# Lag products of two neighbouring channels at once, 64 rows by 40 columns, with reordered channels and a new instruction order

## The chip, the core and the metric

The kernel runs on one core of a Trainium2 chip. The metric is the device time of one execution in microseconds; lower is better. The core has a matrix engine (PE, with its weight loads listed as PEld), a vector engine (DVE), a scalar engine (ACT), GpSimd (POOL) and the SP queue, which in this kernel issues all transfers, one after the other.

## The reference

Two branches are computed from the same input x (2048 tokens, 512 channels) and mixed by a gate.

```
g = sigmoid((x * gate_w).sum(-1, keepdims=True))
a = attention(x)      # 32 heads of 16, 4 segments of 512: causal softmax inside a segment,
                      # plus a linear memory of the segments before; then @ wo
b = ssm_conv(x)
out = g * a + (1 - g) * b

# ssm_conv, for each of 512 channels d, with 128 complex states n:
dt = exp(log_dt);  A = A_re + 1j*A_im;  dB = dt * (B_re + 1j*B_im);  C = C_re + 1j*C_im
P[d,n,l] = exp(dt*A * l)
K[d,l] = real( sum_n C[d,n] * P[d,n,l] * dB[d,n] )         # a kernel of 2048 lags
y = causal convolution of x and K along the tokens (by FFT) + x * Dskip
```

The lags l are bfloat16 numbers in the reference, so only some of the 2048 differ.

## The kernel before, in words

**Order.** The program first builds a list of 1853 operations, each with its engine, its function and its dependences. A long string, `ORDER`, then says in which order they are put on the engines' queues, which buffer each takes, and for moves out of PSUM whether ACT (mark `a`) or DVE (mark `v`) does them. `replay` assigns the buffers, `emit` works out the semaphore waits. Every engine runs its own list strictly in that order; transfers all stand in SP's list.

**Attention.** For each segment s and group hg of eight heads: projections to q and k, scores in five pieces (A0, B0, C, A1, B1), each 128x2048, that always use PSUM banks 0 to 3, one exponential for each piece on ACT (80 in all, L1080), products with v, a division, the memory's part, and a transposition. The other four banks serve all other work.

**Lag kernel.** `ssm_prep` transposes the six parameter arrays (three products of eight transposes, moved out of PSUM by `evac`) and computes z = exp(dt*A); `ssm_powers` squares it nine times; `ssm_cb` makes C*dB (and, with Dskip, a diagonal). `tables(c)`, for each group c of 128 channels, builds by complex products on DVE (L1175, L1178, L1182) two tables: F with the powers z^f for 20 exponents and G with C*dB*z^g for 32 exponents. The wanted values are K at lag f+g = sum over n of G[n,g]*F[n,f] for every channel: the *lag products*. States n lie on the 128 partitions, so each channel is one product with 32 columns of weights (G) and 20 moving columns (F), for the real and the imaginary part added up in PSUM. Four channels run in four strips of 32 columns of the array (`tile_position`). Half of a group's results fill one bank; `evac` moves them to the tile `kex`, and four transfers of 40 KB bring `kex` into `KTT`, from which the spectra are made. A table stores channel pairs next to each other: its place is `(dl//2)*2*N + 2*e + dl%2` for channel dl and exponent e.

**Convolution.** `x_level1` transforms x and writes it to memory (`Zd`). `tail(half)`, for channels 0 to 255 (a) and 256 to 511 (b) and each of 16 frequency groups t: load constants (CT 192 KB, CD 320 KB) and a slice Zx, product X, swap of its halves by two transfers, product K from `KTT` and CD, product Y on DVE, inverse product V, and a transfer into V2. At the end, for 16 token groups, products with wo and the last inverse step are added in PSUM and mixed by DVE (L1331, L1336), then stored.

All matrix products are recorded at the helper's line L698, moves out of PSUM at L226 (ACT) and L227 (DVE), transfers at L222.

Of the kernel before, what the change touches and what calls it, by code (L numbers as in the profile page):

```python
# [7 lines left out]
ACT = mybir.ActivationFunctionType  # L8
# [358 lines left out]
15/0 9/0 10/1 205/0 0/0 23/0/1 24v 29/0 30/0 31/10 193/0 33/7 54/1 57/5 21/0 189/0 1/0 14/2 1226/0 38/1 34 7/0  # L367
1234/4/0 1244/1/1 12/1 35 36 39/2 37/3 32/4 45/7 1242/2 44/5 13/4 11/3 40/6 46/8 190 41 17/0 20/0 58v/0 1232/3 55/7
27/5/0 42 43 50/12 48/0 47 1245a 18/0 5/0 191 61/1 16/0 59/0 51/13 62v/0 60 63 49/9 25/6/2 71/0 588/0 56a 196/0 73/2
53/0 2/0 72 83/1 52 200/1/0/0 85/3 26v 84 74v/2 1233a 98v/1 97/4 1235a 65/2 3/0 95/1 250/7/1/1 391/1 212/6 66/5 197/0  # L370
96 86v/3 67 201a 87 1243a 1246 109/3 64 107/3 108 122v/4 110a/5 77/0 6/0 213a 121/6 251a 28v 202 75 79/7 99 1247/1 88
1236 119/1 203/2/0 100 76 173/0 120 204a 176/2 219/0/1 220 198/0 174/3 131/1 178/1 589/3 175/0 994v/0 252 133/2 590
132 78 134v/6 221 255/2/0/1 253/0/1 240/0/0 111 112 241 256 257 192/0 377/0 996v 143/3 1310/0 1260/3/1 144/4 254a 997v
145 206/1 242 177 157/3 91/0 208/2 228/0/2 995v 229 1000/1 181/1 155/0 1261a 999 1258/0 123 124 199/0 1012/0 179/3 156
209a 214/3/1/0 210/2 230 1001 158v/7 1005 998v/0 159 1002 1003/1 1004 207a 211a 146v/8 223/0/3 224 1248/1/0 135 160
1259a 225 89/2 167v/9 258 1250/2 147 1249a 168 1009/1 222/0 1251a 136 236/0/1 4/0 237 148 226 227 235/1 169 231 1011
337/2/2 90 1013 1008 232/3 1020 1021/0 238 262/0/3 103/6 215 263 1252 338a 1262 101/0 233 1227/2/0 239 216 1022 102
264 1010 243 234/0 244 217 1265/3/1 1014 1015/0 245/4 115/1 1228a 113/2 266/0/2 1023 267 1229/0 246 1024/1 114
293/2/2/2 1266a 268 265/3 247 799/0 1016 271/0/1 272 592/0 1025 294a 1230a 1006/0 8/0 800/1 273 1231 383/0/0/0 384a
269 1237/2/0 125/0 279/0/0 280 801 295 1017 1018/1 378/0 379 270 274 1007 275/0 1019 1263/1 1032 127/4 1033/0 281  # L380
296/0/0 283/0/3 284 1264a 276 1267 297a 1238a 381 285 1026 1239/1 334/2/1/1 1255/0/1 335a 1240a 307/0/2 308 218/2/0
259 1256a 278/1 277/1 1034 309 1029 1027/1 1030/0 282 286 287 1253/0 1268/0 1241 1254a 298/3/1/0 260/0 299 1031 1035
303/0/1 1036/0 304 1028 443/0/1 305 1286/2/0 802 1287a 320/0/0 321 1037 126 1043/2/1 1044 1045 380 444a 1289/1 1257
288/1 137/2 1046 139/2 300 138 1047v 339/0/0/1 398/3 194 289 151/3 385 322 340 312/0/3 1290/2/1 313 180 399a 341 290
1292/3 248/0 149/0 182 249v/0 314 1293v 1038/1 1039 150 336 1040 1041 1056a/0 1053v/0 1055v 1052v 1054v 1058/1 342
1057 306/0 1284/3 1291a 1042a 1285a 591 324/0/1 325 310 311 291/2 386/1/0 315 382/1 1288 1059 1274/3/0 1070/0 68v/0
1063 1060 1061/1 1062 69 1066 1294 1067/1 104v/2 326 346/0/2 347 387a 319/1 323 327 328 329/2 1051/0 80v/1 316/5 1069
292a 348 396/2 1068 1073/1 330 350/0/3 1275a 351 1276/3 397a 1071 1300/2/1 352 317 1078 355/0/0 152a/5 331/1 1072 81
1277a 356 1302/1 349/3 353 1278 1079/0 1301a 318 1281/2/0 1279/0 357 363/0/1 364 354 358 1303a 1074 116v/4 105 106
1076/1 1080 153 1081 92a/7 392/1 365 393a 1282a 1280a 1075 359/1 367/0/2 368 70 1082/0 1304 93 369 360 1283 490/1/2/2  # L390
1271/2/1 301 361/0 1272a 94 302/0 1084 1083 1269/3 154 405/0/3 406 1077 343 1050 22/0 1090 1048 362/2 366 370 1270a
1307/3/0 1091/0 371 1049 1273 344 1088/1 407 447/0 332/0 1092 409/0/0 410 1087 1089 1064/0 491a 117 118 82 1308a 394/1
1065 411 1297/3/1 333a 395a 1085/1 372/3 422/0/2 423 1298a 1295/0 408/1 412 1094/0 1093 1305/3 1296a 1095 424 1086
140v/6 440/0/1/1 388/0 163/0 389 141 1330/0 1306a 441a 1317/1 426/0/3 427 1101/3/0 1299 1096/0 1097 1102 1103 1104 373
195 374 164a/3 448/2/1/0 1309 165 492 128v/9 345 390/1 261 428 414/0/1 1105a 161/2 449 450 415 493/3/2 416 413 1098
1099 494a 1100a 1318/0 1331/1 1113a/0 1319/0 162 442 472/0/0 473 1332/1 1358/2 417 142 129 421/2 425 429 1320/3/0 474
170v/8 171 451 375/0 430 1108 130 1321a 1114v/0 1111v 1119/0 1118 1110v 1112v 1120 1115 1116/1 1109 376a 455/0/1 418/4
1117 1106 166 1128/0 1125/1 1323 1107 1124 1121 431/0 456 457 1322 1127 1126 1333/3/2 541/0/0 1129 1131/1 1136 542a
1122/0 543/1 1130 459/0/2 460 172 1345/1 461 419 432 1132 1324/0/0 1325a 433/0 464/0/3 1137/1 1334a 465 803 458/0
1326/0 1344/0 462 1327/2/0 1138 466 400/3/0/1 463 1371/0 420 1328a 401 476/0/1 1134/1 1133 471/1 477 467 1335 1336  # L400
# [1039 lines left out]
```

## Time and profile before

| | |
|---|---|
| median of 3 runs | 306.34 us (306.05 to 309.47) |
| the profiled execution | 307.74 us |
| its span, first to last instruction | 305.9 us |
| PE busy | 255.6 us (84%) |
| DVE busy | 277.6 us (91%) |
| ACT busy | 256.9 us (84%) |
| mean granted PE clock | 0.964 |
| moved by transfers | 47.91 MB |

Busy time is the time in which at least one instruction of the engine was in flight; on PE it counts the length of pipelined products and is no measure of how full the array was. Times in the rows are microseconds from the start of the span, except means, which are nanoseconds.

### The profile page before, as it was taken

Reading aid. Unit: us, or ns where it says so; the run is one execution under the profiler, and the core shown is the slowest. Engines: PE = TensorE matmul, PEld = TensorE weight load, DVE = VectorE, ACT = ScalarE, POOL = GpSimd, SP = SyncE. Lnnn points to the kernel's source line nnn. Section 1 sums busy time; section 2 is a strip of 40 time slices with the busy share of each in tenths; the row PEclk is TensorE's granted clock in tenths of the full one; section 3 lists DMA queues with packets and bytes.
Section 4 is the critical chain, followed back from the end, with each engine's and each line's share of the span. In section 5 each row is a group of like instructions: output and inputs, shape, how many; then the busy total and the mean of one; then the engine's idle time right before and its main releaser. Section 6 shows DMA issues by size and latency. Waiting matters only on the chain.

```text
span 305.9 us, 10281 instructions
## 1 busy us (share of the span) xinstructions
PE 255.6 (84%) x4334; PEld 177.4 (58%) x4367; DVE 277.6 (91%) x690; ACT 256.9 (84%) x305; POOL 3.3 (1%) x10
## 2 busy tenths in 40 slices
PE   1667779888777859998999998999999998899990
PEld 1423335546453636677666675677577666688870
DVE  1999996999999889999999988898899899989992
ACT  2899997999999987887999999899999999993000
POOL 2000000000000000000000000000000000000000
PEclk9999975999799998999999999999999999999996
DMA  6996361432133723564655557667686676742243
GB/s 150 286 181 164 72 155 36 139 105 79 51 93 88 247 67 121 132 190 142 188 168 175 183 168 216 204 189 222 201 257 185 194 249 197 246 113 81 88 150 91
DMA packets 55502, 47.91 MB, mean 157 GB/s; under 512 B 22688, under 2 KB 50336, under 8 KB 55456
## 3 DMA queue, kind: packets, MB, share of 16 engines
q1 hardware_dynamic: 55456, 47.26, 52.9%
q8 instruction: 34, 0.56, 0.8%
q14 instruction: 12, 0.10, 0.1%
HBM read 29.02 MB, written 6.29 MB: 115 GB/s over the span
## 4 chain that ended last, share of the span: by engine, by line
ACT 40%; PE 25%; DVE 18%; DMA 7%; issue 4%; SPq 4%; DVEq 0%
PE psum L698 24%; ACT sb L1080 22%; ACT sb L226 11%; SPq L222 4%; DVE sb L1336 4%; DVE sb L1331 3%; DMA sb<-c_DNM 3%; ACT sb L806 3%; DVE sb L1285 2%; DMA sb<-sb 2%; DVE sb L1175 2%; DMA sb<-in_A_x_dram 2%; DVE sb L1178 1%; DVE sb L1182 1%; DVE sb L227 1%
## 5 line engine op out<-in xcount | busy, mean ns | idle before, releaser
L698 PE MATMUL psum<-sb 128*128 128x17 bf16 (+10 forms) x4246 | 249.3, 224 | 35.5 <-ACT sb L1080 19.4
L698 PEld LDWEIGHTS psum<-sb 128*128 128x128 bf16 (+3 forms) x4279 | 171.1, 96 | 111.6 <-ACT sb L1080 36.0
L1080 ACT ACTIVATE sb<-psum 128x2048 bf16<-128x2048 f32 x80 | 151.4, 1892 | 4.0 <-PE psum L698 3.4
L226 ACT ACTIVATE sb<-psum 128x512 bf16<-128x512 f32 x156 | 88.2, 611 | 14.1 <-PE psum L698 13.7
L1175 DVE TENSOR_TENSOR sb<-sb 128x512 bf16<-128x512 bf16 (+3 forms) x52 | 34.0, 662 | 1.4 <-DMA sb<-sb 1.4
L227 DVE CAST sb<-psum 128x512 bf16<-128x512 f32 (+1 forms) x46 | 30.8, 674 | 4.0 <-PE psum L698 3.5
L1178 DVE TENSOR_TENSOR sb<-sb 128x512 bf16<-128x512 bf16 (+3 forms) x52 | 34.0, 659 | 0.0
L1182 DVE TENSOR_TENSOR sb<-sb 128x512 bf16<-128x512 bf16 (+3 forms) x52 | 33.7, 664 | 0.2
L1092 DVE TENSOR_TENSOR sb<-sb 128x1024 bf16<-128x1024 bf16 (+1 forms) x40 | 22.8, 580 | 2.0 <-ACT sb L1080 1.7
L1285 DVE TENSOR_TENSOR sb<-sb 128x1024 bf16<-128x1024 bf16 x32 | 21.7, 679 | 1.3 <-ACT sb L226 0.7
L1331 DVE SCALAR_TENSOR_TENSOR sb<-sb 128x256 f32<-128x256 bf16 x32 | 14.2, 480 | 0.3 <-DMA sb<-in_A_x_dram 0.3
L1055 DVE TENSOR_TENSOR sb<-psum,sb 128x256 bf16<-128x256 f32 x32 | 13.3, 417 | 0.3
L1336 DVE SCALAR_TENSOR_TENSOR sb<-psum,sb 128x256 bf16<-128x256 f32 x32 | 13.3, 479 | 0.0
L806 ACT ACTIVATE sb<-sb 128x512 f32<-128x512 f32 x18 | 11.7, 658 | 0.0
L1052 DVE RECIPROCAL sb<-psum 128x16 f32<-128x16 f32 x32 | 7.9, 248 | 0.9 <-PE psum L698 0.9
L227 DVE COPY sb<-psum 128x1024 bf16<-128x1024 bf16 x4 | 2.7, 687 | 6.3 <-PE psum L754 6.3
L1132 DVE TENSOR_TENSOR sb<-psum,sb 128x512 bf16<-128x512 f32 x12 | 8.2, 687 | 0.2
L960 ACT ACTIVATE sb<-psum 128x512 bf16<-128x512 bf16 x12 | 7.4, 615 | 0.4 <-PE psum L957 0.4
L1011 ACT ACTIVATE sb<-sb 128x512 bf16<-128x512 bf16 x12 | 7.6, 633 | 0.0
L807 DVE TENSOR_TENSOR sb<-sb 128x256 f32<-128x256 f32 x18 | 7.5, 423 | 0.0
L808 DVE SCALAR_TENSOR_TENSOR sb<-sb 128x256 f32<-128x256 f32 x18 | 7.4, 414 | 0.0
L754 PE MATMUL psum<-sb 128*128 128x128 bf16 x24 | 2.6, 290 | 5.3 <-DMA sb<-c_ident 5.3
(67 smaller groups left out, 102.2 us busy)
## 6 DMA issues: line engine op xcount, KB each, us to landing
sb<-c_DNM SPq DMA_DIRECT2D x32, 320.0 KB, 3.7
sb<-c_DNM SPq DMA_DIRECT2D x32, 192.0 KB, 2.9
sb<-sb SPq DMA_DIRECT2D x84, 64.0 KB, 2.6
sb<-in_A_x_dram SPq DMA_DIRECT2D x9, 512.0 KB, 4.6
scr_Z<-sb SPq DMA_DIRECT2D x16, 256.0 KB, 2.3
sb<-scr_Z SPq DMA_DIRECT2D x32, 128.0 KB, 3.2
sb<-sb SPq DMA_DIRECT2D x32, 128.0 KB
out_dram<-sb SPq DMA_DIRECT2D x8, 256.0 KB, 2.2
```

Of the source, the lines that this page charges most:

```text
L226: fa = lambda e: e.activation(dst(), src(), ACT.Copy)
L227: fd = lambda e: e.tensor_copy(dst(), src())
L698: mm = lambda e, o_, l, r_, st, sp, **kw: e.matmul(o_, lhsT=l, rhs=r_, start=st, stop=sp, skip_group_check=True, **kw)
L806: op("ACT", ("As", 512), lambda e, sq=sq, Z=Z: e.activation(ap(sq, n=512), ap(Z, n=512), ACT.Square), r=[Z], w=[sq], key=PW[h] + PWS * k)
L1080: o = op("ACT", ("Ax", 2048), lambda e, P=P, pT=pT: e.activation(ap(pT, n=2048), ap(P, n=2048), ACT.Exp, scale=0.25), r=[P], w=[pT])
L1092: op("DVE", ("V2", 128 * nb), lambda e, pT=pT, dims=dims: e.tensor_tensor(ap(pT, dims=dims + [[1, 128]]), ap(pT, dims=dims + [[1, 128]]), ...
L1175: op("DVE", ("V2" if n > 1 else "V1", 256 * n), lambda e: e.tensor_tensor(run(tile, ne, dst, 1), run(tile, ne, src, sstep), ap(pw, cl * 51 ...
L1178: op("DVE", ("V2" if n > 1 else "V1", 256 * n), lambda e: e.tensor_tensor(run(t2, n, 0, 1), run(tile, ne, src, sstep), ap(pw, cl * 512 + 2 ...
L1182: op("DVE", ("V2" if n > 1 else "V1", 256 * n), lambda e: e.tensor_tensor(D_(), D_(), ap(t2, n * 128, [[-n * 128, 2], [2 * n, 64], [1, 2 * ...
L1285: op("DVE", ("V2", 1024), lambda e, Y=Y, XAB=XAB, K3=K3: e.tensor_tensor(ap(Y, dims=[[512, 2], [1, 512]]), ap(XAB, dims=[[512, 2], [1, 512 ...
L1331: op("DVE", ("V1", 256), lambda e, xd=xd, b4=b4: e.scalar_tensor_tensor(ap(xd, n=256), ap(xns[b4 // 4], (b4 % 4) * 512 + half * 256, n=256 ...
L1336: op("DVE", ("V1", 256), lambda e, ou=ou, b2=b2, j=j, b4=b4, P=P, xd=xds[j]: e.scalar_tensor_tensor(ap(ou, (2 * b2 + j) * 256, n=256), ap( ...
```

## The change

- A lag product now takes a pair of neighbouring channels: 64 columns of weights (32 exponents of both channels, contiguous) and 40 moving columns (20 exponents of both). The result is 64 by 40, of which the halves that mix the two channels are not wanted. Two pairs run in two strips of 64 columns. There are 512 products instead of 1024, with twice the result columns.
- A group fills four PSUM banks, eight channels each, instead of two. `evac` moves a bank with both column parities, 320 elements on each partition, so there are 16 such moves instead of 8. The wanted half is picked by the transfers out of `kex`, which read every second partition. `kex` is twice as large, with one buffer instead of two.
- So that the picked half lies as before, the channels are reordered in the tables: in each block of 64, places 2s and 2s+1 hold channels s and 32+s. The move of the transposed parameters, the exponential of log_dt, the load of Dskip (now four) and the diagonal row carry that order.
- `ORDER` is another list with 1864 operations (not shown: 97 lines). Nearly all neighbourhoods are alike, but many operations stand some places earlier or later, and 80 moves out of PSUM or copies are new or on another engine than before; of the lag moves 13 are on ACT and 3 on DVE (5 and 3 before).

```
-    kexP = mkpool("kex", 1280, 2)
+    kexP = mkpool("kex", 2560, 1)
...
-    S.dma(lambda: ap(dskT, n=4), lambda: B_Dskip.rearrange("(k p) -> p k", p=128), 1024, w=[dskT], key=9, slow=True, q=LQ)
+    for j in range(4):
+        S.dma(lambda j=j: ap(dskT, n=4, p0=64 * (j // 2) + j % 2, np_=32, pstep=2), lambda j=j: B_Dskip.rearrange("(k p) -> p k", p=128)[32 * j:32 * j + 32, :],
+              256, pw=[dskT], key=9, slow=True, q=LQ)
...
-            S.evac(lambda T=T: ap(T, n=1024), lambda P=P: ap(P, n=1024), 1024, r=[P], w=[T], psum16=True)
+            S.evac(lambda T=T: ap(T, dims=[[64, 16], [1, 2], [2, 32]]), lambda P=P: ap(P, dims=[[64, 16], [32, 2], [1, 32]]), 1024, r=[P], w=[T], psum16=True)
...
-        op("ACT", ("Asx", 512), lambda e: e.activation(ap(dt, n=512), ap(ldt, n=512), ACT.Exp), r=[ldt], w=[dt])
+        op("ACT", ("Asx", 512), lambda e: e.activation(ap(dt, dims=[[64, 8], [1, 2], [2, 32]]), ap(ldt, dims=[[64, 8], [32, 2], [1, 32]]), ACT.Exp), r=[ldt], w=[dt])
...
-        for hf in range(2):
+        for b in range(4):
             P = S.ps()
-            for sl0 in range(0, 16, 4):
-                def f(e, P=P, hf=hf, sl0=sl0):
-                    for sl in range(sl0, sl0 + 4):
+            for s0 in range(8 * b, 8 * b + 8, 4):
+                def f(e, P=P, b=b, s0=s0):
+                    for s in range(s0, s0 + 4):
                         for cc in range(2):
-                            for dq in range(4):
-                                dl = 32 * dq + 16 * hf + sl
-                                i = mm(e, ap(P, sl * NF, n=NF, p0=32 * dq, np_=32), ap(G, (1 - cc) * GPL + (dl // 2) * 2 * NG + dl % 2, [[2, NG]]),
-                                       ap(F, cc * FPL + (dl // 2) * 2 * NF + dl % 2, [[2, NF]]), cc == 0, cc == 1, tile_position=(0, 32 * dq))
+                            for h in range(2):
+                                i = mm(e, ap(P, (s - 8 * b) * 40, n=40, p0=64 * h, np_=64), ap(G, (1 - cc) * GPL + (32 * h + s) * 2 * NG, n=64),
+                                       ap(F, cc * FPL + (32 * h + s) * 2 * NF, n=40), cc == 0, cc == 1, tile_position=(0, 64 * h))
                     return i
-                op("PE", c_pe("C", *[20] * 8), f, r=fr + gr + [F, G], pw=[P], acq=[kex])
-            S.evac(lambda hf=hf: ap(kex, 16 * hf, [[32, NF], [1, 16]]), lambda P=P: ap(P, dims=[[1, NF], [NF, 16]]), 320, r=[P], pw=[kex])
+                op("PE", c_pe("C", *[40] * 4), f, r=fr + gr + [F, G], pw=[P], acq=[kex])
+            S.evac(lambda b=b: ap(kex, 8 * b, [[640, 2], [32, NF], [1, 8]]), lambda P=P: ap(P, dims=[[1, 2], [2, NF], [40, 8]]), 320, r=[P], pw=[kex])
         for dq in range(4):
             S.dma(lambda dq=dq: ap(KTT, (4 * c + dq) * 160, n=160),
-                  lambda dq=dq: ap(kex, n=640, p0=32 * dq, np_=32), 40960, r=[kex], pw=[KTp[c // 2]])
+                  lambda dq=dq: ap(kex, dq % 2 * 640, n=640, p0=64 * (dq // 2) + dq % 2, np_=32, pstep=2), 40960, r=[kex], pw=[KTp[c // 2]])
...
-    S.evac(lambda: ap(drowT, n=512), lambda: ap(PR, n=512), 512, r=[PR], w=[drowT], key=200)
+    S.evac(lambda: ap(drowT, dims=[[64, 8], [32, 2], [1, 32]]), lambda: ap(PR, dims=[[64, 8], [1, 2], [2, 32]]), 512, r=[PR], w=[drowT], key=200)
```

More of the change, by code (lines that the diff above doesn't have):

```diff
@@ new lines @@
+1505a 708a 656 662/2/1/1 625 457 626 627 631 1598/0 1490 1500/1/2 663 1489 1501a 664 807/1 604/1 555 636/0/3 603
+1624/2 1221/3 1222 1483 989/0 1524/1 1224/1 1223v 188 1512/0 1503 1502 637 1225 704/2/1/0 1226a 1493/0 632/2 686/0/2
+687 1494/3/0 547 596/0 633 665 634/0 1517/1/1 638 635/0 639 1470 669/0/1 1518v 1510/1 1420/0 1622/2 1609/4 1234 705v
+1235 1495a 643 1506/1 644 1530/1/0 645/3 646 670 647 706 1531a 671 1507/2/1 673/0/3 1513/3/0 1508a 585/0/4/0 1419/0
+819/2 1514v 614/3/0/0 586 1596/0 1515 1623/0 587 588 1236 1509 674 734/0/0 1233 820v 615 1525/1 672/0 735 1516
```

179 lines of the change are left out of this document (87 added, 92 removed).

## The prediction, on record before the result was known

> **What bounds the kernel now.** I read the page first, then the busy time by stage, then the chain of waits and the groups by shape.
>
> ```profile
> span 305.9 us, 10281 instructions
> PE 255.6 (84%) x4334; PEld 177.4 (58%) x4367; DVE 277.6 (91%) x690; ACT 256.9 (84%) x305; POOL 3.3 (1%) x10
> ACT 40%; PE 25%; DVE 18%; DMA 7%; issue 4%; SPq 4%; DVEq 0%
> 0.00:24.00 24.00, 11.99 (x106) 7.41 (x108) 17.39 (x51) 17.36 (x33) 1.98 (x8) 1.00 0.84 207
> 24.00:100.00 76.00, 60.30 (x1089) 34.88 (x1101) 72.76 (x185) 73.56 (x94) 0.65 (x1) 0.91 0.35 98
> 100.00:165.60 65.60, 57.82 (x1175) 41.50 (x1169) 61.99 (x151) 57.02 (x73) 0.00 (x0) 0.97 0.54 159
> 165.60:272.20 106.60, 100.14 (x1729) 71.63 (x1739) 98.71 (x240) 103.75 (x103) 0.66 (x1) 1.00 0.66 201
> 272.20:300.10 27.90, 25.33 (x268) 22.00 (x266) 26.77 (x68) 5.24 (x7) 0.00 (x0) 1.00 0.37 112
> ```
>
> The last five rows are stretches of the span; after the length come the busy times of PE, PEld, DVE, ACT and POOL. I cut at the starts of the 24th, the 40th and the 80th exponential (L1080) and at DVE's last work. No engine is the bound of the whole: from 24 to 100 us ACT is idle for 2.4 us and DVE for 3.2; from 100 to 165.6 DVE paces (3.6 idle, ACT 8.6); from 165.6 to 272.2 ACT paces (2.9 idle, DVE 7.9); at the end DVE (1.1 idle). The last 5.8 us are the way out of the last stores. A microsecond added to the pacing engine of a stage is worth about one, on another engine less.
>
> How the ACT stages run:
>
> ```profile
> 73.58 0.97 ACT sb L226 x2
> 74.55 1.78 ACT sb L1080
> 269.82 1.88 ACT L1080 ACTIVATE sb<-psum 128x2048 bf16<-128x2048 f32 x1
> 272.20 1.88 ACT L1080 ACTIVATE sb<-psum 128x2048 bf16<-128x2048 f32 x1 [0.50 <-PE psum L698]
> 265.17 0.70 DVE sb L227
> 266.20 0.60 DVE sb L227
> ```
>
> A PSUM move of 512 costs ACT 0.97/2 = 0.48 and DVE 0.60 when others follow. All exponentials use the same four PSUM banks, so with nothing put between them two of them stand 2.38 apart, 0.5 of it idle.
>
> **The lag products.** They are the 32-column products:
>
> ```profile
> L698 PE MATMUL psum<-sb 128*32 128x20 bf16 x1024 | 10.1, 177 | 1.1 <-issue 0.9
> L698 PE MATMUL psum<-sb 128*128 128x17 bf16 x1280 | 44.2, 171 | 0.5 <-DVE sb L227 0.2
> 64.14:65.15 1.01, 1.01 (x127) 1.00 0.27 95
> 74.19:75.18 0.99, 0.99 (x42) 1.00 0.24 57
> 102.98 1.11 PE psum L698 x25
> 136.18 3.30 PE psum L698 x124
> 140.84 2.07 PE psum L698 x134
> 180.73 4.80 PE psum L698 x190
> ```
>
> The window at 64.14 holds only lag products: 127 in 1.01 us, 8.0 ns each. Four of them, in four column strips, stand side by side, so a round of four takes 32 ns; 1024 are 256 rounds, 8.2 us. The window at 74.19 holds the 17-column products that use the whole array, and there one takes 0.99/42 = 24 ns. After the change there are 512 products but only two side by side: again 256 rounds. So the halved count doesn't halve the time. The new round (64 columns of weights, 40 moving) is not in the trace. From below it is bounded by 24 ns (6.1 us in all), from above by transposes with 128 columns of weights and 128 moving:
>
> ```profile
> 118.34 0.39 PE L957 MATMUL psum<-sb 128*128 128x128 bf16 x4
> L957 PE MATMUL psum<-sb 128*128 128x128 bf16 x48 | 4.7, 219 | 0.2
> ```
>
> Four take 0.39 of which the last itself lasts 0.22, so they start 57 ns apart (14.6 us in all). The 17-column row is the nearer in moving size: I take 27 ns, 6.9 us, a gain of 1.3. Only part lies on the chain: the groups quoted at 102.98, 136.18, 140.84 and 180.73 have 473 products, by the shapes some 380 of them lag products (3.0 us); a sixth of that is **-0.5**, at 24 ns -0.7, at 57 ns +2.3.
>
> The Trainium skill (TensorEngine Tiling, Overview and Tiling Modes) speaks against the change: a weight width up to 32 lets four column tiles run, up to 64 two, so twice the width is half the tiles; by it the PE time stays 8.2 us and the term is 0. The trace agrees with the four-fold half of it (8.0 ns each).
>
> **The additional PSUM moves.** Half of each product is thrown away, so a channel group fills four banks instead of two: 16 moves of 320 instead of 8.
>
> ```profile
> L226 ACT ACTIVATE sb<-psum 128x320 bf16<-128x320 f32 x5 | 2.3, 457 | 0.4 <-PE psum L698 0.4
> L227 DVE CAST sb<-psum 128x320 bf16<-128x320 f32 x3 | 1.5, 487 | 0.1
> L226 ACT ACTIVATE sb<-psum 128x512 bf16<-128x512 f32 x150 | 85.3, 614 | 13.6 <-PE psum L698 13.3
> L227 DVE CAST sb<-psum 128x512 bf16<-128x512 f32 x43 | 29.3, 688 | 3.9 <-PE psum L698 3.5
> L227 DVE COPY sb<-psum 128x1024 bf16<-128x1024 bf16 x4 | 2.7, 687 | 6.3 <-PE psum L754 6.3
> ```
>
> The order's marks say which engine takes each: ACT 13 instead of 5, DVE 3 as before. Of the 457 ns some 0.13 overlap the next instruction as in the 512 row (614 against 0.48), so ACT gets 8 x 0.32 = 2.6. The new order pays with other moves: of those of 512, DVE takes 50 instead of 43 (+4.2), ACT 143 (-3.3); one of 1024 and two small copies go the other way. Over the kernel DVE gets +3.1, ACT +0.9.
>
> By stage, counting between the same three exponentials in both orders with these prices: before the 24th ACT +0.3, DVE -0.9; from there to the 40th ACT +3.0, DVE +2.3 (a table product is drawn forward); to the 80th ACT -1.9, DVE +2.3; behind it DVE -0.6. Taking the pacing engine of each stage: **+0.3**, **+2.3**, then a choice, then **-0.6**. In the third stage ACT paces, but its 1.9 us less don't come back whole: three exponentials now follow another with nothing between, one before, at 0.5 idle each, and others get less than 0.5 between them; summed as the larger of 2.38 and 1.77 plus what stands between, ACT's road from the 40th to the 80th is 103.5 before and 103.7 after. Bounds: -1.9 and DVE's +2.3; I take **+0.9**, nearer to ACT.
>
> **The reordering in the tables.** The parameter moves now write every second element. On DVE 1024 bf16 take 687 ns, as long as 512 f32, so two elements pass at a time; if the step breaks that, one of them takes about 0.6 more. Three moves: one goes to ACT, one has time, the first is on the path of the start: 0 to +0.6, **+0.4**. The exponential of dt and the diagonal row are written or read with a step by engines that already take one element at a time: nothing, else some tenths. The Trainium skill (VectorE: DVE Perf Modes, What auto-detection actually checks) has the paired mode only for 16-bit tensors with step 1; by it the term would be the full +0.6. No step of two in such a move is in this trace.
>
> **The queue.** One small load of Dskip becomes four:
>
> ```profile
> 90.61 0.60 SPq L222 DMA_DIRECT2D sb<-in_B_Dskip_dram  x1
> 8.39 2.32 SPq L222 DMA_DIRECT2D sb<-in_gate_w_dram  x1
> 111.88 0.60 SPq L222 DMA_DIRECT2D sb<-sb  x1
> sb<-sb SPq DMA_DIRECT2D x1, 40.0 KB, 1.9
> 113.91 4.60 PE L698 MATMUL psum<-sb 128*128 128x256 bf16 x54 [1.95 <-ACT sb L1080]
> 116.23 1.09 ACT L226 ACTIVATE sb<-psum 128x512 bf16<-128x512 f32 x2 [2.36 <-PE psum L698]
> 112.79 0.69 DVE L1175 TENSOR_TENSOR sb<-sb 128x1024 bf16<-128x1024 bf16 x1 [1.36 <-DMA sb<-sb]
> 116.86 0.69 DVE L1285 TENSOR_TENSOR sb<-sb 128x1024 bf16<-128x1024 bf16 x1 [0.73 <-ACT sb L226]
> ```
>
> Three more issues of 0.6 on SP; one of them and the load of gate_w (2.3) now stand ahead of the input x of the first transform. What is queued behind them (x, wq, wk) is needed around 13 to 17 us; x would be issued near 8 us and take 4.6, just in time. Nothing for that, as ACT and DVE have the powers' chain to do until then; 1 us if it is late.
>
> The other rows are a wait that the order removes. The only 40 KB transfer in the window from 111.86 is the last lag move of group 1; issued at 111.88, landed 1.9 later, at 113.8, and PE starts the first kernel spectrum (K, half a) at 113.91 after 1.95 idle. ACT and DVE wait for that (2.36, 0.73); DVE's 1.36 wait is for a power's copy from the same queue. Before, that last move stood behind the swap of the first X; now the four stand ahead of it, so that after the last PSUM move near 106 they are issued by about 109.7 and land by 111.6; the power's copy stands earlier too. DVE gets back 1.36 + 0.73: **-2.1** (0 if another transfer is late instead, -2.4 with ACT's).
>
> Against this, constants come later in the new order.
>
> ```profile
> sb<-c_DNM SPq DMA_DIRECT2D x32, 192.0 KB, 2.9
> PEld psum L698 <- DMA sb<-c_DNM: 1.5, 2, 0.9
> PE psum L698 <- DMA sb<-c_DNM: 1.4, 3, 0.8
> ```
>
> The 192 KB loads land after 2.9; 8 of 32 have under 1 us of ACT's and DVE's work between the place of their issue and their product, before 3. The shortfalls of all transfers of the tail against their landing times add up to 52 instead of 42, a quarter more; a quarter of the waits above and of the like, **+0.4** (0 to +2). The single kex buffer costs nothing: groups are over 25 us apart and a lag transfer lands in about 2; the four moves out of it still carry 40 KB each.
>
> **Sum.** 0.3 + 0.4 + 2.3 - 2.1 - 0.5 + 0.9 - 0.6 + 0.4 = +1.1. The profiled execution took 307.74 (its span 305.9 and 1.8 around it), which makes 308.8; it lies 1.4 above the median of the runs, 306.34, from which the forecast is **307.4**. Bounds of the terms, all at one end: -3.0 and +10.2.
>
> **Rivals.**
> - *Constants late.* The place is PE's wait at the X products of the tail. Five more loads are issued at their use; at 2.9 each that is 14.5, with half covered by products already queued +7, instead of 0.4: 314.0. For it: SP is one queue in order and stands behind waits. Against it: in the trace PE and PEld wait only 2.9 in all for c_DNM, though 12 loads were close already. It decides once such waits pass about 8 us.
> - *DVE takes every stage.* Then the +2.3 of the third stage counts in full and the removed wait returns elsewhere: 307.4 + 1.4 + 2.1 = 310.9. For it: DVE is 91% busy and gets 3.1 more. Against: 7.9 idle in the third stage.
> - *The new order is simply tighter.* ACT's -1.9 comes back, -2.4 at 113, no other wait, and nothing for steps and constants: 307.4 - 2.8 - 0.3 - 0.8 = 303.5. For it: ACT has less to do where it paces. Against: the three exponentials with nothing between.
> - *No gain on PE.* A round of two stays 32 ns or more, up to 57: +0.5 to +2.8, 308 to 310; it is inside the forecast's range.
>
> **Chances.** Forecast (with the last rival) 0.50, constants 0.13, DVE 0.19, tighter 0.18. Two per cent, about what a measurement of this kernel tells from no change, are 6.1 us: 300.2 to 312.5. Beyond the upper end lie most of the first rival and little of the second, 0.15; below the lower end a tail of the tight order, 0.06; within 0.79. Range 302.5 to 313.0; the forecast's own 305 to 310.
>
> **What would show it.** Lag products: 512 in about 7 us, pairs 27 ns apart. The 320 moves: 13 on ACT at 0.46, 3 on DVE at 0.49. Parameter moves on DVE at 1.1 to 1.3 instead of 0.69. No wait near 114 us ahead of the first K. DVE busy near 280. It is wrong if the exponentials from the 40th to the 80th take over 110 us, if PE waits over 8 us for c_DNM, or if a round of lag products passes 50 ns.

## The result and the profile after

| | before | after |
|---|---|---|
| median of 20 runs, us | 306.76 (304.92 to 309.47) | 304.69 (303.27 to 306.36) |
| ratio, 95% interval | | 0.9922 [0.9899, 0.9945] |
| profiled execution, us (span) | 307.74 (305.9) | 304.81 (303.0) |

The change is 0.8% faster, 2.1 us. The forecast was 307.4, 0.3% slower than the median known then: its sign was wrong, its range (302.5 to 313.0) held the time. On another chip the change itself came out at 0.9948 [0.9910, 0.9985]. The ratios compare undisturbed executions alone, so a ratio need not be the quotient of two medians over all executions.

The page of after, then the stretches cut at its own 1st, 24th, 40th and 80th exponential and at VectorE's last work:

```profile
span 303.0 us, 9317 instructions
PE 260.7 (86%) x3855; PEld 176.8 (58%) x3855; DVE 280.6 (93%) x694; ACT 258.4 (85%) x309; POOL 3.3 (1%) x10
PE 31%; DVE 27%; ACT 26%; DMA 5%; issue 5%; SPq 4%; DVEq 0%; ACTq 0%
```

```profile
0.00:25.55 25.55, 12.47 (x88) 6.88 (x89) 19.79 (x56) 18.43 (x32) 1.98 (x8) 0.98 0.85 209
25.55:99.94 74.39, 64.12 (x923) 35.15 (x923) 72.49 (x184) 73.31 (x92) 0.65 (x1) 0.89 0.34 96
99.94:163.22 63.28, 57.38 (x981) 41.54 (x981) 61.09 (x140) 59.48 (x81) 0.00 (x0) 1.00 0.59 166
163.22:269.50 106.28, 101.59 (x1608) 71.08 (x1606) 101.17 (x251) 102.51 (x101) 0.66 (x1) 1.00 0.69 205
269.50:296.97 27.47, 25.11 (x268) 22.15 (x266) 26.06 (x66) 4.64 (x6) 0.00 (x0) 1.00 0.31 92
```

Set against the same five stretches of before (24.0, 76.0, 65.6, 106.6 and 27.9 long), the 24th exponential comes at the same time, and the stretch to the 40th is 2.3 us shorter. VectorE's columns say how. It works 3.0 us more in all, and is idle 16.4 us up to its last work instead of 22.5 (by stretch 5.8, 1.9, 2.2, 5.1, 1.4 after; 6.6, 3.2, 3.6, 7.9, 1.1 before). More work and less waiting: -6.1 + 3.0 and 0.2 more at the end is the -2.9 of the spans.

The groups that the change touches:

```profile
L698 PE MATMUL psum<-sb 128*64 128x40 bf16 x512 | 9.2, 186 | 0.1
L226 ACT ACTIVATE sb<-psum 128x320 bf16<-128x320 f32 x13 | 5.5, 466 | 0.4 <-PE psum L698 0.3
L227 DVE CAST sb<-psum 128x320 bf16<-128x320 f32 x3 | 1.5, 486 | 1.0 <-PE psum L698 1.0
L226 ACT ACTIVATE sb<-psum 128x512 bf16<-128x512 f32 x143 | 81.9, 624 | 8.2 <-PE psum L698 7.8
L227 DVE CAST sb<-psum 128x512 bf16<-128x512 f32 x50 | 33.5, 682 | 1.5 <-PE psum L698 1.3
L227 DVE COPY sb<-psum 128x1024 bf16<-128x1024 bf16 x3 | 3.2, 1083 | 1.0 <-PE psum L756 1.0
```

The third field is the idle time ahead of the group. Ahead of ScalarE's 512 moves it fell from 13.6 to 8.2, ahead of VectorE's from 3.9 to 1.5; ahead of the lag products from 1.1 (0.9 of it "issue") to 0.1.

One warning on the pair of profiles. The granted clock in 40 slices, of before, of after, and of an experiment (e8 below) whose program is that of before up to about 95 us:

```profile
PEclk9999975999799998999999999999999999999996
```
```profile
PEclk9997978999996999999999999999999999999996
```
```profile
PEclk9998879999999997999999999999999999999996
```

Before's profile was granted 0.7 and 0.5 in its slices from 38 to 53 us, and its 21st exponential starts at 89.6; the same program starts it at 87.3 in e8 and at 88.2 in e17. So the profile of before stands about one microsecond above its median (307.74 against 306.76), and of the 2.9 us between the two spans some 2 are the change's.

A second difference of clock lies where the change gains most. The clock falls to half for 3.4 us or a multiple of it, at other places in other executions. In before's profile it is half from 113.5 to 116.9 us, in that of after nowhere between 99.5 and 297:

```profile
103.05:117.40 14.35, 10.07 (x188) 6.26 (x189) 11.54 (x36) 11.78 (x15) 0.00 (x0) 0.88 0.36 99
102.95:114.64 11.69, 8.56 (x126) 5.29 (x125) 11.46 (x35) 11.65 (x17) 0.00 (x0) 1.00 0.60 161
```

These are the stretches from the 25th to the 29th exponential, before and after; the third figure from the end is the granted clock. Three traces in the order of after that have 3.4 us of half clock between 107 and 117 us (e3, e15, e16 below) take 63.0 to 64.2 us from the 24th to the 40th exponential, against 63.3 in after and 65.6 in before. So most of the 2.3 us stays when both have such a stretch, but a difference of one or two microseconds between two single traces can be the clock alone.

### The profile page after: what moved, and what is told of

The parts are those of the page before. It is cut to its first block, busy times and chain, and to the rows that moved or that the text cites. A ratio compares the mean times of both kernels' runs of the same rounds, so it can differ in the third digit from the quotient of the medians.

```text
span 303.0 us, 9317 instructions
## 1 busy us (share of the span) xinstructions
PE 260.7 (86%) x3855; PEld 176.8 (58%) x3855; DVE 280.6 (93%) x694; ACT 258.4 (85%) x309; POOL 3.3 (1%) x10
## 4 chain that ended last, share of the span: by engine, by line
PE 31%; DVE 27%; ACT 26%; DMA 5%; issue 5%; SPq 4%; DVEq 0%; ACTq 0%
PE psum L698 30%; ACT sb L1082 11%; ACT sb L226 10%; DMA sb<-sb 4%; SPq L222 4%; DVE sb L1337 4%; DVE sb L227 4%; DVE sb L1332 3%; DVE sb L1286 3%; DVE sb L1094 3%; ACT sb L808 3%; DVE sb L1177 2%; DVE sb L1184 2%; DVE sb L1180 2%; DMA sb<-in_B_log_dt_dram 1%
## 5 line engine op out<-in xcount | busy, mean ns | idle before, releaser
L698 PE MATMUL psum<-sb 128*128 128x17 bf16 (+11 forms) x3767 | 254.7, 233 | 24.0 <-ACT sb L1082 11.7
L226 ACT ACTIVATE sb<-psum 128x512 bf16<-128x512 f32 (+2 forms) x158 | 88.9, 618 | 8.6 <-PE psum L698 8.1
L227 DVE CAST sb<-psum 128x512 bf16<-128x512 f32 (+1 forms) x53 | 34.9, 671 | 2.4 <-PE psum L698 2.3
L1094 DVE TENSOR_TENSOR sb<-sb 128x1024 bf16<-128x1024 bf16 (+1 forms) x40 | 22.5, 573 | 0.4 <-ACT sb L1082 0.4
L756 PE MATMUL psum<-sb 128*128 128x128 bf16 x24 | 2.7, 279 | 5.0 <-DMA sb<-c_ident 4.6
L959 PE MATMUL psum<-sb 128*128 128x128 bf16 x48 | 4.9, 227 | 2.2 <-ACT sb L226 2.2
```

Source lines behind the costliest of these rows:

```text
L226: fa = lambda e: e.activation(dst(), src(), ACT.Copy)
L227: fd = lambda e: e.tensor_copy(dst(), src())
L698: mm = lambda e, o_, l, r_, st, sp, **kw: e.matmul(o_, lhsT=l, rhs=r_, start=st, stop=sp, skip_group_check=True, **kw)
L1094: op("DVE", ("V2", 128 * nb), lambda e, pT=pT, dims=dims: e.tensor_tensor(ap(pT, dims=dims + [[1, 128]]), ap(pT, dims=dims + [[1, 128]]), ...
```

## The experiments

Two theories at the outset. **A**: the new order alone brings the gain, the products nothing. **B**: the products bring it, on TensorE. Start of some exponentials in the traces, to place each gain and loss (us):

| | 1st | 21st | 25th | 29th | 33rd | 37th | 80th | span |
|---|---|---|---|---|---|---|---|---|
| before | 24.2 | 89.6 | 103.1 | 117.4 | 131.7 | 154.1 | 272.2 | 305.9 |
| after | 25.6 | 89.2 | 103.0 | 114.6 | 130.5 | 151.5 | 269.5 | 303.0 |
| e1 old products, new order | 25.3 | 89.3 | 105.4 | 117.6 | 133.0 | 159.7 | 278.1 | 311.4 |
| e9 the same, half the products | 25.0 | 88.0 | 101.3 | 112.8 | 128.6 | 149.6 | 269.8 | 303.2 |
| e12 after, two transfers back | 25.4 | 88.9 | 102.6 | 114.2 | 132.2 | 153.2 | 270.9 | 304.4 |
| e17 before, two transfers forward | 24.4 | 88.2 | 101.7 | 114.3 | 128.6 | 150.7 | 268.2 | 302.2 |

### Products and order taken apart (e1, e2)

```diff
 e1: ORDER of after, operations of before
-lag%d: 8 x 16 products of 64x40, 4 moves of 320
+lag%d: 8 x 32 products of 32x20, 2 moves of 320
```
(Where the expectations below speak of moves of 640, read 320: before has two of 320 in a group, after four.) In e1 the two old moves of a group stand where the later of two new ones stood; the parameter moves are unstepped.

> The operations of before (32 by 20 lag products, 8 moves of 320, unreordered tables, one Dskip load) put into the order of after; two lag banks of after's order become one half of before's. Theory A (the order alone gives the gain, the new products cost nothing or a little): 303.5 to 304.7, at or under after's 304.7, since 8 moves of 320 (2.6 us of ACT) and two slow parameter moves (1.2 us of DVE) are gone. Theory B (the pair products themselves give the gain): back at 306 to 307.5.

Measured: 313.29 (311.36 to 315.53), ratio 1.0243 [1.0188, 1.0298]. Both theories missed, by 6 us. The group of the lag products and two of TensorE's waits in e1:

```profile
L698 PE MATMUL psum<-sb 128*32 128x20 bf16 x1024 | 9.9, 178 | 8.1 <-issue 8.0
```
```profile
104.19 2.57 PE L698 MATMUL psum<-sb 128*32 128x20 bf16 x41 [2.31 <-issue]
144.75 1.53 PE L698 MATMUL psum<-sb 128*32 128x20 bf16 x78 [3.69 <-issue]
```

While its span exceeds that of after by 8.4 us, TensorE waits 8.0 us in the middle of lag products for nothing that the profile shows ("issue"). The two need not be the same microseconds: e1 also had half the clock for 13.6 us between 105.8 and 150.1, and e5 below loses 2.9 us of such waits and hardly any time. In before the same group had 0.9 of it, in one place:

```profile
104.97 2.85 PE L698 MATMUL psum<-sb 128*32 128x20 bf16 x108 [0.88 <-issue]
```

The queue for instructions gives the reading (first row before, second after; transfers, MB, share):

```profile
q8 instruction: 34, 0.56, 0.8%
```
```profile
q8 instruction: 30, 0.49, 0.7%
```

0.56 MB in 34 transfers is 16 KB each; PE and PEld have 4334 + 4367 instructions, 256 to a transfer. By the packets of this queue, a transfer ended at 102.86 and 143.23 in e1, at 103.67 in before, at 103.84 in e8, at 144.89 in e4; TensorE went on 1.33, 1.52, 1.30, 1.25 and 1.29 us later. An old lag product and its weight load pass every 8.0 ns, so 256 instructions last 1.0 us; the transfer alone takes 0.9 to 1.4 in before and e1. I call this theory **S**: where short products stand close, TensorE is out of instructions. The Trainium skill (Advanced Engine Details and Errata, ISA Cache) has instructions come in lines of 16 KB, 256 of them; the 34 transfers here agree, and what running dry costs only the trace shows.

The other half of the cross, new products in the old order:

```diff
 e2b: ORDER of before, operations of after
-move of 320 of a lag half
+move of 320 on ScalarE right behind its products, another where the old one stood
```

> The operations of after put into the order of before: the two banks of a half one after the other, their additional moves on ACT just ahead of the old ones, the four Dskip loads at the place of the one; 32 operations slip by a few places for want of a free buffer. Theory A: slower than before by 1 to 3 us (307.5 to 310), as only costs are added. Theory B: 304 to 305.5.

A first build measured 326.35, 1.0655 [1.0605, 1.0706]; 32 operations had slipped in it for want of free PSUM banks, and it tells nothing. The second build, with none slipped:

> The new products (64 by 40, two channels at once, 16 moves of 320 columns, stepped parameter moves) in the order of before, every lag run cut where before cuts it; each former move of 640 becomes one of 320 on ScalarE right after its products and one of 320 where the move of 640 stood. Theory S (half as many instructions per microsecond spare TensorE the wait of 1.05 us at 104 us, the rest of the gain is the order): before less about 1.0 and plus 0 to 0.7 for the stepped moves and the added moves, 305.0 to 306.4 us, ratio 0.994 to 0.999, no gap over 0.2 us inside a lag run. Theory O (all of the gain is in the order, the products bring none): 306.5 to 308.5 us, ratio 1.001 to 1.008.

Measured: 314.51, 1.0270 [1.0227, 1.0312]: both missed again. No "issue" wait is left at its lag products; the waits are for moves.

```profile
L699 PE MATMUL psum<-sb 128*64 128x40 bf16 x512 | 11.5, 191 | 1.9 <-ACT sb L226 1.6 <-DVE sb L227 0.2
```

```profile
66.05 0.44 ACT L226 ACTIVATE sb<-psum 128x320 bf16<-128x320 f32 x1 [0.99 <-PE psum L699]
104.10 0.77 ACT L226 ACTIVATE sb<-psum 128x320 bf16<-128x320 f32 x2 [1.03 <-PE psum L699]
```
```profile
67.62 0.42 DVE L810 TENSOR_TENSOR sb<-sb 128x256 f32<-128x256 f32 x1 [1.22 <-ACT sb L809]
```

ScalarE stands in front of an added move until its products are done, and VectorE behind ScalarE. So neither half, as built, gives the gain: new in new 304.7, old in old 306.8, the two mixtures 313.3 and 314.5. Theory A falls with e1. B isn't tested fairly: e2b shows what the added moves cost where ScalarE must wait for them, and not what the products would bring in an order made for them.

### Is it instructions? (e4, e5, e8, e9, e10, e11, e13, e14)

e4, in after, each lag product issued twice:

```diff
-for s in range(s0, s0 + 4):
+for s in [v for v in range(s0, s0 + 4) for _ in range(2)]:
```

> After, with each lag product issued twice into the same place (the second overwrites the first with the same numbers): 8.2 us more of PE. If the lag products lie beside other work: +0 to +1 us. If about 3.0 of their 8.2 us lie on the path, as the prediction took from the chain: +2.5 to +3.5 (307 to 308). If all: +8.

Measured: 316.13, 1.0324 [1.0272, 1.0375], the span 11.2 us longer, about the 8.2 us of TensorE time and 2.9 of "issue" together, as if more work in the lag groups lay fully on the path. The waits (0.68 and 2.26 us) also show that at 16 ns a product TensorE runs out too, when twice as many follow each other:

```profile
L698 PE MATMUL psum<-sb 128*64 128x40 bf16 x1024 | 18.5, 189 | 3.0 <-issue 2.9
```

e5 cuts the long runs of e1, e8 the long run of before:

```diff
 e5, groups 1 and 2           e8, group 1
 lag products 128              lag products 96
+two other PE operations      +a state's products
 lag products 128              lag products 96
```

> The old products (64 rows by 20 columns, four channels at once) in the new order as in the run of old products in the new order (313.3 us, 1.024 of before), with one edit: the lag runs of groups 1 and 2, there 256 products on end, are cut into 128 and 128 with two other TensorE operations between them. Theory S (the loss of 8.4 us came from TensorE running out of instructions inside long runs of short products): most of the 3.9 us at 145 us and of the 2.6 us at 104 us comes back, 305 to 309 us, ratio 0.998 to 1.010, and the gaps inside the lag runs add up to under 4 us (8.9 there). Rival O (the new order only fits the new products: moves of 640 columns where two of 320 were planned): at least 312 us, ratio over 1.018, with short gaps or not.

> Before, with one edit: the lag run of group 1 of 192 products on end is cut into 96 and 96, with the products of one state and one score block between them. Theory S (TensorE's wait of 1.05 us inside that run is a wait for instructions, and lies on the path): no gap over 0.3 us there, 0.5 to 1.1 us less than before, ratio 0.996 to 0.9985. Rival (the wait is hidden by VectorE, or the waits behind it take it back): ratio 0.999 to 1.002 though the gap is gone.

Measured: e5 313.12, 1.0224 [1.0170, 1.0278]; e8 307.93, 1.0052 [1.0017, 1.0086]. Both cuts failed to do what they were made for:

```profile
L698 PE MATMUL psum<-sb 128*32 128x20 bf16 x1024 | 10.2, 177 | 5.2 <-issue 5.1
```
```profile
105.09 2.85 PE L698 MATMUL psum<-sb 128*32 128x20 bf16 x108 [2.65 <-issue]
```

e5 still waits 5.1 us and keeps nearly all its loss, though 2.9 us of waiting are gone; e8 waits 2.65 at one place, more than before did. In e1, e5 and e8 the wait sits at the same place of TensorE's own stream, at the 2735th, 2735th and 2733rd instruction shown, whatever stands around it. A few operations between two runs don't thin out the instructions of the microseconds around a boundary; to read this as a matter of unbroken runs alone was wrong. (In e5 about a dozen neighbouring operations, one lag move among them, also changed their place at each cut.)

e9 (e1), e10 (before) and e11 (after) leave out the half of the products that adds the second part of each complex sum:

```diff
-for cc in range(2):
+for cc in range(1):
```

> The old products in the new order (313.3 us, 1.024 of before), with the second half of the lag products left out (the lags are then incomplete): 512 products of 64 rows by 20 columns instead of 1024, the same moves, order and waits. Theory S (its loss of 8.4 us against the change comes from TensorE running out of instructions where 64 products stand on end eight times, since two instructions go every 8 ns): with half as many the gaps inside the lag runs are under 1 us in all, and the time falls by 6 us or more, to 303 to 307 us, ratio 0.988 to 1.002. Rival O (moves of 640 columns and their order do it): it falls by the 4.1 us of TensorE time at most, to 309 us or more, ratio over 1.008.

> Before, with the second half of the lag products left out (512 of 1024). Theory S (the wait for instructions at 104 us delays the last move of group 1, its transfer and the table operation that VectorE waits for at 113 us): the last move of group 1 comes by 104 us instead of 105.7, VectorE's wait near 113 us falls under 0.5 us, and the time falls by 3.0 to 5.5 us, ratio 0.982 to 0.990. Rival (TensorE's 4.1 us in the lag groups are hidden by VectorE and ScalarE, stall and all): by less than 2.5 us, ratio over 0.992.

> The change, with the second half of the lag products left out (256 of 512 products of 64 rows by 40 columns, 4.1 us of 8.2). Theory P (TensorE's time in the lag groups lies on the path here as its doubling showed, 11.2 us for 8.2): 2.0 to 4.5 us less than the change, ratio to before 0.977 to 0.987. Rival (less TensorE time is hidden, more is not): 0.988 to 0.993. Either way the half of before should gain more than this one if the wait for instructions counts there.

Measured: e9 303.19, 0.9910 [0.9874, 0.9945]; e10 303.44, 0.9917 [0.9876, 0.9957]; e11 304.94, 0.9957 [0.9921, 0.9993]. The lag groups of e9 and of e11:

```profile
L698 PE MATMUL psum<-sb 128*32 128x20 bf16 x512 | 5.0, 177 | 0.1
```
```profile
L698 PE MATMUL psum<-sb 128*64 128x40 bf16 x256 | 5.6, 188 | 0.6 <-DVE sb L227 0.6
```

e9 is the plainest result of the study: 10.1 us for 4.1 us of TensorE time, the "issue" wait gone from 8.0 to 0; theory S as foretold, and rival O out, since the moves and their order are those of e1. Some of the 10.1 may be clock: the median over the executions was 0.972 in e9 and 0.958 in e1, and over the 125 executions of before beside these runs 0.01 less of it goes with 1.2 us more, which makes an estimate of 1.7 us. In after the same halving gives nothing measurable (theory P fell): 4.1 us less TensorE time there is hidden, though 8.2 more were not. In before it gives 2.5 us by the ratio (3.3 by the medians), between the band of S (0.982 to 0.990) and that of its rival (over 0.992). S's further claim there, that the stall causes VectorE's wait at 113 us, is refuted: the trace of e10, though of a long execution (307.33), has no "issue" wait in its lag products, and VectorE waits all the same:

```profile
112.97 0.69 DVE L1175 TENSOR_TENSOR sb<-sb 128x1024 bf16<-128x1024 bf16 x1 [1.76 <-DMA sb<-sb]
```

e13 and e14 were to keep TensorE's time at half the instructions, in e9 and e10:

```diff
-n=NF ... [[2, NF]]
+n=80 ... [[2, 80]]
```

> The old products in the new order with half of the lag products left out, as before (303.2 us, 0.991 of before; with all of them 313.3), and each of the 512 that are left streams 80 columns instead of 20, so that TensorE works about as long in the lag groups as with all 1024 (the result is not the lags): half the instructions, the whole TensorE time. Theory S (it is the number of short instructions that cost the 10 us, not TensorE's time): 302.5 to 305.5 us, ratio 0.987 to 0.997, no gap over 0.5 us in a lag run. Rival P (it is TensorE's time): 309 us or more, ratio over 1.008.

> Before, with half of the lag products left out (303.4 us, 0.992) and each that is left 80 columns wide instead of 20: half the instructions, about the whole TensorE time of before. Theory S (the 2.5 to 3.3 us that halving gained in before are the instructions): 303 to 304.8 us, ratio 0.986 to 0.995. Rival P (TensorE's time): 305.7 us or more, ratio over 0.998.

Measured: e13 303.14, 0.9911 [0.9873, 0.9948]; e14 304.97, 0.9940 [0.9902, 0.9978]. Inside the bands of S, but e13's group shows that the time wasn't restored:

```profile
L698 PE MATMUL psum<-sb 128*32 128x80 bf16 x512 | 6.0, 201 | 0.0
```

Four times the columns cost 1.0 us in all. So this pair doesn't part time from instructions; that rests on the "issue" waits of e1, which the same products, halved, don't have. (One execution of e14, the profiled one, took 1227.81 us with TensorE busy 96% of it. I have no cause for it, and its trace isn't used.)

### The place of two transfers (e12, e17, e15)

The lines of after that answer to before's wait at 113 us:

```profile
112.23 1.27 PE L698 MATMUL psum<-sb 128*128 128x256 bf16 x10 [0.72 <-DMA sb<-sb]
115.85 0.69 DVE L1286 TENSOR_TENSOR sb<-sb 128x1024 bf16<-128x1024 bf16 x1 [1.34 <-issue]
117.90 1.57 ACT L226 ACTIVATE sb<-psum 128x512 bf16<-128x512 f32 x3 [1.38 <-PE psum L698]
108.79 2.59 SPq L222 DMA_DIRECT2D sb<-sb  x4
```

The first K starts at 112.23 instead of 113.91, and VectorE's and ScalarE's next waits are as long as the old ones. Did the earlier transfers bring anything? e12 puts them back in after, e17 brings them forward in before:

```diff
 e12 (after)                        e17 (before)
-pwc1.9 lag1[2] lag1[3] X Z X       -lag1[0] pwc1.5 lag1[1] lag1[2] pwc1.8 X lag1[3] X
+lag1[2] X lag1[3] Z X pwc1.9       +pwc1.8 lag1[0] pwc1.5 lag1[1] lag1[2] lag1[3] X X
```
(pwc is a power's copy, X a swap of the first X, Z a Z tile.)

> The change, with two of its transfers put back to where before has them: the last of the four lag transfers of group 1 behind the first swap of X, the copy of a power behind the second swap. Theory T (the term of -2.1: VectorE's waits of 1.36 and 0.73 us at 113 and 117 us went because these transfers stand earlier): 1.5 to 2.7 us more than the change, ratio to before 0.997 to 1.002. Rival (what they gained was taken up by the next waits, 1.34 us at 115.9 and 1.38 at 117.9): 0 to 0.6 us more, ratio 0.991 to 0.995.

> Before, with two of its transfers moved forward in the queue: the copy of a power (issued at 109.6 us, for which VectorE waited 1.36 us at 112.8 us) right behind the copy of another power at 104.6, and the last lag transfer of group 1 (issued at 111.9 us, for which TensorE waited 1.95 us at 113.9 us) ahead of the first swap of X. Theory T (these two places are a part of the change's gain and need neither its products nor the rest of its order): VectorE's wait at 113 us under 0.4 us, 1.0 to 2.1 us less than before, ratio 0.993 to 0.997. Rival (the swap of X, now one place later, or another wait takes it back, as happened in the run with the swaps first): ratio 0.998 to 1.003.

Measured: e12 305.66, 0.9959 [0.9923, 0.9994]; e17 306.28 (301.97 to 308.95), 0.9904 [0.9849, 0.9959]. In the traces, e12 then e17:

```profile
114.92 0.69 DVE L1180 TENSOR_TENSOR sb<-sb 128x1024 bf16<-128x1024 bf16 x1 [1.92 <-DMA sb<-sb]
118.71 1.57 ACT L226 ACTIVATE sb<-psum 128x512 bf16<-128x512 f32 x3 [2.67 <-PE psum L698]
```
```profile
103.69 2.85 PE L698 MATMUL psum<-sb 128*32 128x20 bf16 x108 [0.98 <-issue]
111.89 3.30 PE L698 MATMUL psum<-sb 128*128 128x256 bf16 x54 [1.24 <-issue]
113.82 0.69 DVE L1285 TENSOR_TENSOR sb<-sb 128x1024 bf16<-128x1024 bf16 x1 [0.44 <-ACT sb L226]
```

Put back, VectorE's wait for a transfer returns (1.92). Brought forward, the wait of 1.36 is gone, though the stall of 0.98 ahead of it stands. This part of theory T is shown from both sides: with before's places VectorE waits 1.36 to 1.92 us for a transfer here in all five traces (before, e7, e8, e10, e12), with the earlier places in none of five (e17, after, e3, e11, e16).

What the wait is worth isn't shown. e12 loses 2.2 us on after from the 29th to the 33rd exponential, and e17 wins 1.8 us on before from the 25th to the 29th, but the clock differs at just these places. First e12 and after, then e17 (before's row stands above):

```profile
114.16:132.23 18.07, 15.99 (x215) 11.63 (x213) 16.05 (x35) 14.58 (x19) 0.00 (x0) 0.81 0.49 137
114.64:130.49 15.85, 14.02 (x215) 10.52 (x212) 14.51 (x33) 14.34 (x19) 0.00 (x0) 1.00 0.58 160
```
```profile
101.68:114.26 12.58, 8.94 (x196) 5.90 (x197) 11.35 (x36) 11.68 (x15) 0.00 (x0) 1.00 0.42 116
```

e12 had half the clock from 116.3 to 123.1, and the same 215 products were busy 2.0 us longer; e17 had full clock where before had half. The times don't settle it either: e12's interval overlaps that of after, and e17's ratio rests on the six shortest of its twelve executions, while the median of all twelve is 306.28 against 306.56 beside it. e8, 2.3 us early at the 21st exponential, is 1.2 early at the 25th (its stall is 1.8 longer) and level with before at the 29th, behind the same wait for the transfer (1.43).

e15 goes on in after: the swaps of X ahead of a power's copy, a Z tile and a constant.

```diff
-constant  pwc1.9  lag1[2]  lag1[3]  X swap  Z tile  X swap
+lag1[2]  lag1[3]  X swap  X swap  pwc1.9  Z tile  constant
```

> The change, with the queue's order mended at one place: the two swaps of the first X (issued at 110.8 and 112.0 us) go ahead of a power's copy, a Z tile and a constant's load, each of which takes the queue 0.6 us. If VectorE's wait of 1.34 us at 115.9 us hangs on these (theory Q), that wait falls under 0.4 us and 0.5 to 1.5 us are won on the change. Rival: the power's copy is late in its place and takes the gain back, as its later place cost 1.4 us of the span in the run with transfers put back: between 0.3 us less and 0.7 us more than the change.

> The change itself, unaltered, beside the others on one chip: 304.0 to 305.2 us, ratio 0.989 to 0.995.

Measured: e15 304.94, 0.9969 [0.9935, 1.0003]; e16, the change itself beside it, 304.60, 0.9948 [0.9910, 0.9985]. VectorE's 1.34 at 115.9 is gone and another has come, the rival:

```profile
113.83 0.69 DVE L1181 TENSOR_TENSOR sb<-sb 128x1024 bf16<-128x1024 bf16 x1 [0.74 <-DMA sb<-sb]
```

### The start (e3, e7)

```diff
 e3 (after): SP's queue           e7 (before): VectorE's queue
+load of log_dt                   -gate3 read, scale, 2 table ops, gate1 read, 4 ops
 load ...                         +scale, 2 table ops, gate3 read, 4 ops, gate1 read
-load of log_dt
```

> After, with the load of log_dt put first in the transfer queue (it is fifth) and nothing else changed. At the head ACT's exponential of log_dt waited 3.5 us for it and DVE 0.9 us; the first attention exponential stood at 25.55 instead of 24.22. Theory that a late head is worth its length at the end: 303.4 to 304.0. Theory that it is absorbed by 60 us (the 12th exponential was already level with before): 304.4 to 304.9, no difference that can be told.

> Before, with one edit: VectorE's reads of the products of gates 3 and 1, for which it waited 1.43 us at 48.5 us and 1.26 us at 52.4 us, stand two and four table operations later in its queue. Theory A (VectorE's lateness from there lasts through the stretch from 61 to 100 us, which VectorE fills, and so to the end; this is part of the gain of the change): 0.8 to 2.2 us less than before, ratio 0.993 to 0.997. Rival (later waits take it back): ratio 0.998 to 1.002.

Measured: e3 305.95, 1.0006 [0.9974, 1.0038], its first exponential later still (26.2); e7 308.25, 1.0040 [1.0003, 1.0076]. Nothing is won at the start by either. VectorE's waits at 48 and 52 us, which e7 was to remove, were largely that execution's clock: e8, with the order of before there, waits 0.49 at the first and not at the second.

```profile
47.72 0.16 DVE L898 TENSOR_SCALAR sb<-psum 128x4 f32<-128x4 f32 x1 [0.49 <-PE psum L698]
```

## Why the prediction was wrong

Its terms against the profile (the first two stretches of before's profile are 1 to 2 us longer than in e17 and e8):

| term | forecast | measured |
|---|---|---|
| start, stepped parameter moves | +0.4 | first exponential +1.3 (25.55 for 24.22) |
| to the 24th exponential | +0.3 | 0 with the start's in this pair; +1.3 against e17, which has before's order up to there |
| 24th to 40th, VectorE's added work | +2.3 | VectorE works 0.9 less there |
| wait at 113 us removed | -2.1 | the wait is gone; VectorE's idle time from the 24th to the 40th -1.4 |
| lag rounds | -0.5 | 0 |
| 40th to 80th | +0.9 | -0.3 |
| tail | -0.6 | -0.4 |
| constants | +0.4 | no wait for them left (1.4 on TensorE before) |

**The step that failed** is "By stage, counting between the same three exponentials in both orders". Its count of ScalarE's work was near (+3.0 forecast, +2.5 measured from the 24th to the 40th), and VectorE's total was near: 3.0 us more, of which some 1.2 are the two stepped moves that the prediction priced apart, so 1.8 for its 3.1. VectorE's place was wrong: up to the 24th exponential it did 2.1 us more where -0.9 (+0.3 with the two stepped moves) stood in the sum, and to the 40th 0.9 less where +2.3 stood.

The count took VectorE's place beside the exponentials from the written order. Set against the traces, that place is off. VectorE's operations ahead of an exponential:

| | listed ahead, before / after | begun in the trace, before / after |
|---|---|---|
| 24th | 244 / 242 | 235 / 239 |
| 40th | 384 / 385 | 384 / 379 |
| 80th | 623 / 629 | 623 / 629 |

Each engine runs its own list, so VectorE can lag behind the place that the common list gives it. In before it was 9 operations (2.8 us of work) behind at the 24th exponential and had caught up at the 40th; in after it was 3 behind (1.0 us) and then 6 (1.6 us). So before did work between the two that after had done already or still left over. This goes with the order and not with how long VectorE had waited: at the 24th exponential all five traces with the order of before have begun 234 or 235 operations (before, e7, e8, e10, e17) and all six with that of after 238 or 239 (after, e3, e11, e12, e15, e16), though e8 had waited 7.9 us by then and before 9.9. Why the lag differs in the two orders is not shown.

From the 40th to the 80th exponential VectorE's 2.5 us more, forecast as 2.3, went into its idle time (7.9 to 5.1), and the stretch grew by none of it. With -0.9 in the place of +2.3 the sum would be -2.1, the change of the medians; that it fits so well is luck, as other terms miss in both directions. The result, 304.7, lies nearest to the rival "The new order is simply tighter", given 0.18 at 303.5.

**The lag products.** In after, a stretch that holds only lag products:

```profile
99.83:101.88 2.05, 2.05 (x129) 2.05 (x128) 1.32 (x4) 1.94 (x2) 0.00 (x0) 1.00 0.41 105
```

129 in 2.05 us are 16 ns each, 32 ns a round, not 27: no TensorE time is won, as the rival "No gain on PE" and the quoted rule of the Trainium skill (TensorEngine Tiling, Overview and Tiling Modes) had it. The choice of the row "nearer in moving size" was wrong: in e13 four times the moving size added a fifth. What the halved count does bring stood in a row that the prediction quoted and didn't price, "1.1 <-issue 0.9": instructions come in pieces, and half as many per microsecond don't run out. In before TensorE waited 0.9 us for that (1.2 and 2.65 in e7 and e8); with the old products in the new order it waited 8.0.

**The wait at 113 us** was the right mechanism for its first part: the 1.36 hung on the place of the two transfers. The 0.73, and ScalarE's 2.36 that the prediction read beside it, lie in before's stretch of half clock, where the 54 products of K took 4.60 us and in e17, at full clock, 3.30; so they hang on the clock too. New waits of 1.34 and 1.38 followed in after, and VectorE's idle time in the whole stretch fell by 1.4, not by 2.1.

**The stepped moves.**

```profile
5.66 1.28 DVE L227 COPY sb<-psum 128x1024 bf16<-128x1024 bf16 x1 [0.95 <-PE psum L756]
```

1.28 against 0.69, as the rule of the Trainium skill cited in the prediction (VectorE: DVE Perf Modes, What auto-detection actually checks) had it: the step costs the pairing. The start lost more than its +0.4; what of that reaches the end is not shown, though the 2.3 us that e8 was early at the 21st exponential were gone by the 29th.

**Constants late** did not happen: before's two rows of waits for c_DNM (1.5 and 1.4) have no counterpart in after, whose trace shows no wait for these loads.

**What stays open** is the split of the 2 us. The removed wait is VectorE's 1.36, but its worth in time isn't parted from the clock; halving the products brings 2.5 us in before and nothing in after, without a clear share of the instructions in it; the start costs 1.3 at the first exponential. Before itself scatters by 5 to 8 us over its runs on one chip, more than any of these. Before with both the two transfers and fewer instructions was not tried.

## What to carry to other kernels

Read the third field of a group for "issue" as well as for engines: in a run of products of a few ns it points at the supply of instructions. Both their pace and their number count: at 16 ns a product after has no such wait, twice as many at the same pace have 2.9 us of it (e4), and a few other operations between two runs took away only 2.9 of 8.0 us (e5).

When an order is rewritten, don't read from the list where one engine stands beside another; count in a trace what each has begun. Set the granted clock of two traces side by side before a difference between them gets a price. And test an order and its operations as a pair: mixed, each of these two lost 7 to 8 us.

## What was not expected of the hardware

TensorE's instructions come by transfers of 16 KB, 256 at a time; where products with their weight loads pass every 8 ns, it stood still for 0.7 to 3.7 us at a time, in the five waits named above until 1.25 to 1.52 us after a transfer's end. Rounds of the lag products take 32 ns both as four strips of 32 by 20 and as two of 64 by 40, and 80 columns instead of 20 added only 1.0 us to the busy time of 512 products. Each of the transfers near 110 us occupies the issuing queue for about 0.6 us (four in 2.59). TensorE's granted clock fell to half for 3.4 us or a multiple of it at a time, at other places in executions of one and the same order, and in e12 the same 215 products were busy 2.0 us longer for 6.8 us of it.
